# A gated attention and Fourier block: low parts by ScalarE and adding DMAs, M in another place, GpSimd's queue in written order

## The chip, the cores and the metric

The kernel runs on one core of a Trainium2 chip. The core has five engines with queues of their own, each of which works in order: TensorE (PE, matrix products, with its weight loads as PEld), VectorE (DVE), ScalarE (ACT), GpSimd (POOL) and SyncE (SP). SP issues most of the DMAs, GpSimd most of the others. Only semaphores order one engine against another. The metric is the time of one execution on the device in microseconds, as the median of several runs. Lower is better.

## The reference

One input x of 2048 rows and 576 columns feeds two branches, and a gate per row mixes them.

```python
x = A_x
g = _sigmoid((x * gate_w).sum(-1, keepdims=True))
# A: linear attention, 32 heads of 18, phi(t) = where(t > 0, t + 1, exp(t)) + 1e-6
q, k, v = split(x @ wqkv)
kv  = einsum("bhsd,bhse->bhde", phi(k), v);   z = einsum("bhsd->bhd", phi(k))
num = einsum("bhqd,bhde->bhqe", phi(q), kv)
den = einsum("bhqd,bhd->bhq",  phi(q), z)[..., None] + 1e-6
a = (num / den).reshape(B, S, D) @ wo
# B: the real part of a two-dimensional Fourier transform, by matrices
b = dft_seq_re @ (x @ dft_hid_re.T) - dft_seq_im @ (x @ dft_hid_im.T)
return g * a + (1 - g) * b
```

## The kernel before, in words

All products keep float32 accuracy with a matmul type of lower precision. Each operand is split into a high part (ScalarE copies it into that type, `hi_of`, line 179) and a low part (VectorE subtracts the high part from the original, `lo_of`, line 189). A product is then high by high, high by low and low by high. With `lo_later` the subtraction is put on a list, which `tick` empties further on.

The work goes through these stages, with TensorE busy in each:

1. K's features, phi(x Wk), for 16 tiles of 128 rows, with the gate as an extra column (to about 65 us of the span).
2. The product of x transposed with these features, in five chunks of 128 columns of x and four steps each (lines 739 to 772, `step` counts to 19), and kv from it. V itself is never computed.
3. The q stage (lines 1023 to 1029). Row tiles p and p + 8 form a pair. x's quarters are combined with those of Wq so that seven products give four quarters (PRODUCTS, QP). The combinations of x are a pair's *form* (`forms`, seven pieces with high and low part), and the last 64 columns of x a pair's *remainder* (`rests`, in the profile xr). Some forms were made earlier, stored in DRAM (xm) and come back with `load_forms` (xf); those of pairs 6, 0, 7 and 1 are made on the spot from loaded quarters (xb). `Left.make` is that work in five steps: two of additions, the high part, and the low part in two pieces. The pairs come as (6, 2), (3, 4), (0, 5), (7, 1). There are 56 slots, numbered from 0, and each is one product of seven matmuls, the last with the remainder (line 913). Slot 1 is the first of pair 2, slots 24 and 25 the first of pairs 0 and 5, slot 38 the first of pair 7, slot 41 the first of pair 1.
4. In the same stage M is made. M is kv, masked to the heads, times Wo, so that a = (phi(q) / den) M. It is made in five groups of 126 rows (`build_m`, slots 8 to 12, into mf, at the start of the arena), moved by DMA into chunks of 128 rows (`move_m`), and split into high and low part (`split_m`, whose second argument is the part).
5. The M stage: for each of 16 tiles the normalised q features are transposed (line 828), split (qs) and multiplied with M in 28 matmuls. ScalarE scales the result by the gate, and GpSimd stores it (att). The normalising is `normalise`, a generator whose steps (`pz`, the sum per head, the scaling, a copy into `twice`) are called in slots and tiles. In the same tiles the combined weights Wr are loaded and split (`right_raw`, `make_w`) for the next stage.
6. The Fourier branch, real part and then imaginary part: a hidden product (line 1115) and a sequence product (line 1270).

The dictionary `plan` says behind which slot a piece of work is written, and so do the tuples of numbers behind it: for the making of pairs 7, 0 and 1, the normalising steps (None) and M's parts ("m"). ScalarE and VectorE run in written order from line 556 on (`pace`), SP always does, and TensorE does in the q stage and from line 1393 on. Elsewhere a scheduler sets the order at build time, and for GpSimd it does so in the whole kernel before.

All tiles have fixed places in one arena. A write waits until the last readers of whatever lay there are done. Before, M is moved to T_AT + 25856 (`mraw`), where from 28160 on the `sum` tiles of the first quad lie, and its high part goes to T_AT + 14336, where blocks of Wo lay.

Of the kernel before, what the change touches and what calls it, by code (L numbers as in the profile page):

```python
# [8 lines left out]
F = mybir.dt.float32  # L9
# [127 lines left out]
def kernel(  # L137
# [50 lines left out]
    def lo_of(dst, src, hi):  # L188
        nc.vector.tensor_tensor(out=dst, in0=src, in1=hi, op=ALU.subtract)  # L189

# [365 lines left out]
    pace()  # L556
# [154 lines left out]
    def load_forms(p, o, queue=nc.sync):  # L711
        t = forms[p] = at(o, [P, 7, 2, 2 * P], R, "xf")
        for a, b in ((2, 4), (0, 2), (4, 6), (6, 7)):
            queue.dma_start(out=t.bitcast(F)[:, a:b], in_=xforms[p][:, a:b])

    def load_two(*places):
# [89 lines left out]
    def scale(t, d):  # L806
# [3 lines left out]
        o = (SLOT_AT + (14336 if t < 3 else 48256) if t < 4 else T_AT + 36864) + t % 8 * 512  # L810
# [55 lines left out]
    def move_m(g, queue=nc.sync):  # L866

        if not ms:
            ms["raw"] = at(T_AT + 25856, [P, KC, D], F, "mraw")
            ms["rest"] = at(T_AT + 35072, [P, D], F, "mraw")  # L870
        mraw, mrest = ms["raw"], ms["rest"]
# [13 lines left out]

    def split_m(h, part):
        if h == 0 and part == 0:
            ms["hi"] = at(T_AT + 14336, [P, 5, D], R, "mw")
            ms["lo"] = at(T_AT + 25856, [P, KC, D], R, "mw")
        mraw, mrest, mhi, mlo = (ms[k] for k in ("raw", "rest", "hi", "lo"))  # L890
# [91 lines left out]
    def spread():  # L982
        pz_ring.at = [T_AT + 40960 + k * D * 4 for k in range(4)]

    m_parts = [lambda: split_m(0, 0), lambda: split_m(0, 1),
               lambda: split_m(1, 0), lambda: split_m(1, 1)]
# [19 lines left out]
        31: [lambda: load_rest_q(7, T_AT + 80384, nc.gpsimd),  # L1006
             lambda: load_rest_q(1, T_AT + 108928, nc.gpsimd)],
# [15 lines left out]
    with tc.manual_schedule(engines={mybir.EngineType.PE}):  # L1023
        for k, (n, s, q) in enumerate(slots):
# [3 lines left out]
            if k == 51:  # L1028
                nxt = transposed(0)
# [34 lines left out]
    class Hidden:  # L1064
# [12 lines left out]
        def make_w(self, k):  # L1077
# [6 lines left out]
            lo_later(w[:, :, 1], raw, w[:, :, 0])  # L1084
            lo_later(rl[32:64], last[32:64], rl[32:64])
# [239 lines left out]
    for i, t in enumerate(seq):  # L1325
# [12 lines left out]
        if i == 0 or 2 < i < 7:  # L1338
            go(wr_make)
# [3 lines left out]
        for k, j in enumerate((7, 8, 9, 10, 11, 12, 14)):  # L1343
# [149 lines left out]
```

## Time and profile before

| what | value |
|---|---|
| time of the runs, median (lowest to highest) | 731.05 us (730.86 to 732.08) |
| time of the profiled execution | 731.42 us |
| its span, first to last instruction | 729.62 us |
| mean granted clock of TensorE | 0.997 of full speed |
| TensorE busy | 719.6 us, 99% of the span |
| VectorE busy | 597.3 us, 82% |
| ScalarE busy | 329.6 us, 45% |
| GpSimd busy | 56.8 us, 8% |
| moved by DMA | 156.66 MB, on average 215 GB/s |

Times inside the profile count from the start of the span. A row of the timeline has the start, the length, the engine, the line, the operation, what it writes and reads, how many instructions are joined in it, and in brackets how long the engine was idle before it and what ended that.

### The profile page before, as it was taken

Reading aid. Unit: us, or ns where it says so; the run is one execution under the profiler, and the core shown is the slowest. Engines: PE = TensorE matmul, PEld = TensorE weight load, DVE = VectorE, ACT = ScalarE, POOL = GpSimd, SP = SyncE. Lnnn points to the kernel's source line nnn. Section 1 sums busy time; section 2 is a strip of 40 time slices with the busy share of each in tenths; the row PEclk is TensorE's granted clock in tenths of the full one; section 3 lists DMA queues with packets and bytes.
Section 4 is the critical chain, followed back from the end, with each engine's and each line's share of the span. In section 5 each row is a group of like instructions: output and inputs, shape, how many; then the busy total and the mean of one; then the engine's idle time right before and its main releaser. Section 6 shows DMA issues by size and latency. Waiting matters only on the chain.

```text
span 729.6 us, 13716 instructions
## 1 busy us (share of the span) xinstructions
PE 719.6 (99%) x5390; PEld 715.8 (98%) x5390; DVE 597.3 (82%) x996; ACT 329.6 (45%) x506; POOL 56.8 (8%) x101
## 2 busy tenths in 40 slices
PE   9999999998999999999999999999999999999997
PEld 9999999998999999999999999999999999999997
DVE  5799987577999848979999889857888987788884
ACT  6898346575545544443344334323535332232230
POOL 1111221122041100000000000000000000000000
PEclk9999999999999999999999999999999999999999
DMA  7384798984279648454476666889964544544540
GB/s 255 115 279 163 246 302 296 396 276 175 102 260 384 263 147 329 130 161 137 155 247 175 223 240 199 290 308 400 374 198 132 159 140 141 159 150 144 153 152 33
DMA packets 51516, 156.66 MB, mean 215 GB/s; under 512 B 6212, under 2 KB 8676, under 8 KB 50428
## 3 DMA queue, kind: packets, MB, share of 16 engines
q1 hardware_dynamic: 42268, 116.43, 47.3%
q0 software_dynamic: 8896, 38.95, 14.7%
q8 instruction: 43, 0.70, 0.4%
q10 hardware_dynamic: 288, 0.41, 0.2%
q14 instruction: 21, 0.17, 0.1%
HBM read 117.80 MB, written 36.49 MB: 211 GB/s over the span
## 4 chain that ended last, share of the span: by engine, by line
PE 76%; DVE 10%; DMA 9%; issue 2%; ACT 1%; SPq 1%; POOL 1%; DVEq 0%; POOLq 0%; ACTq 0%
PE bank L1270 41%; PE bank L1115 14%; PE bank L209 14%; DMA xr<-xr 2%; DVE c L189 2%; PE bank L913 2%; PE bank L748 2%; PE bank L571 2%; DVE craw L199 1%; DVE fl L189 1%; DMA wraw<-in_wq_rest_dram 1%; DMA craw<-in_xg_dram 1%; DMA xm<-xb 1%; DVE ys L199 1%; PE bank L828 1%
## 5 line engine op out<-in xcount | busy, mean ns | idle before, releaser
L1270 PE MATMUL bank<-fh,c 128*128 128x288 f32 x1792 | 356.1, 295 | 0.4 <-DVE c L189 0.4
L1270 PEld LDWEIGHTS bank<-fh,c 128*128 128x128 f32 x1792 | 286.0, 188 | 1.0 <-DVE c L189 0.9
L1270 PE MATMUL bank<-fl,c 128*128 128x288 f32 x896 | 263.2, 294 | 0.4 <-DVE fl L189 0.4
L179 ACT ACTIVATE c<-craw 128x1792 fp32r<-128x1792 f32 (+1 forms) x84 | 121.6, 1448 | 192.8 <-DVE craw L199 158.4
L1270 PEld LDWEIGHTS bank<-fl,c 128*128 128x128 f32 x896 | 168.7, 188 | 1.1 <-DVE fl L189 0.9
L189 DVE TENSOR_TENSOR c<-craw,c 128x1792 fp32r<-128x1792 f32 (+4 forms) x86 | 141.9, 1653 | 1.7 <-ACT c L179 1.6
L199 DVE TENSOR_TENSOR craw<-craw 128x256 f32<-128x256 f32 (+1 forms) x192 | 98.3, 512 | 24.3 <-DMA craw<-in_ci_dram 13.0
L1115 PE MATMUL bank<-wf,xf 128*128 128x288 f32 x630 | 98.5, 296 | 0.0
L1115 PEld LDWEIGHTS bank<-wf,xf 128*128 128x128 f32 x630 | 90.0, 189 | 0.0
L209 PE MATMUL bank<-mw,qs 128*128 128x288 f32 x448 | 63.5, 298 | 0.8 <-DVE qs L189 0.5
L748 PE MATMUL bank<-pk,c 128*128 128x288 f32 x448 | 62.1, 296 | 0.8 <-ACT c L179 0.4
L748 PEld LDWEIGHTS bank<-pk,c 128*128 128x128 f32 x448 | 60.1, 188 | 1.5 <-DVE c L189 0.8
L209 PEld LDWEIGHTS bank<-mw,qs 128*128 128x128 f32 x448 | 60.0, 188 | 1.4 <-DVE qs L189 0.7
L209 PE MATMUL bank<-wd,xs 128*128 128x288 f32 (+1 forms) x336 | 44.7, 295 | 0.0
L209 PEld LDWEIGHTS bank<-wd,xs 128*128 128x128 f32 x336 | 44.6, 188 | 0.0
L199 DVE TENSOR_TENSOR ys<-bank,ys 128x288 f32<-128x288 f32 x63 | 28.8, 456 | 17.3 <-PE bank L1270 14.3
L189 DVE TENSOR_TENSOR fl<-fl,fh 128x864 fp32r<-128x864 f32 (+1 forms) x32 | 34.6, 1092 | 6.8 <-ACT fh L179 5.2
L179 ACT ACTIVATE fh<-fl 128x864 fp32r<-128x864 f32 (+1 forms) x32 | 29.8, 949 | 16.2 <-DVE fl L199 16.2
L1115 PE MATMUL bank<-wf,xr 96*128 96x288 f32 x112 | 33.3, 298 | 0.0
L199 DVE TENSOR_TENSOR ys<-ys,bank 128x288 f32<-128x288 f32 x47 | 21.1, 450 | 13.5 <-PE bank L1270 12.9
L1292 ACT ACTIVATE ys<-bank 128x288 f32<-128x288 f32 x16 | 6.6, 412 | 53.2 <-PE bank L1270 53.2
L1333 ACT ACTIVATE acc<-bank,gate 128x288 f32<-128x288 f32 x32 | 15.9, 502 | 29.7 <-PE bank L209 29.6
(131 smaller groups left out, 802.1 us busy)
## 6 DMA issues: line engine op xcount, KB each, us to landing
xf<-xm SPq DMA_DIRECT2D x49, 512.0 KB, 9.0
craw<-in_cr_dram SPq DMA_DIRECT2D x32, 512.0 KB, 3.8
craw<-in_ci_dram SPq DMA_DIRECT2D x32, 512.0 KB, 4.2
xr<-xr SPq DMA_DIRECT2D x20, 448.0 KB, 8.2
xm<-xb POOLq DMA_DIRECT2D x8, 1024.0 KB, 5.2
xm<-xb POOLq DMA_DIRECT2D x8, 768.0 KB, 7.1
craw<-in_xg_dram SPq DMA_DIRECT2D x20, 256.0 KB, 5.9
att<-acc POOLq DMA_DIRECT2D x16, 288.0 KB, 3.5
```

Of the source, the lines that this page charges most:

```text
L179: return nc.scalar.activation(dst, src, AF.Copy, bias=bias)
L189: nc.vector.tensor_tensor(out=dst, in0=src, in1=hi, op=ALU.subtract)
L199: nc.vector.tensor_tensor(out=dst, in0=a, in1=b, op=op)
L209: nc.tensor.matmul(ps, a, b, start=(n == 0), stop=(n == len(pairs) - 1))
L571: nc.tensor.matmul(ps[i], x[:, i * P:(i + 1) * P], wkt.row(h, j), start=(c == 0 and n == 0), stop=(c == KC and n == 1))
L748: nc.tensor.matmul(ps[h][:, :HALF], t[:, a, k], pk[s][:, b, half(h)], start=(s == 0 and n == 0), stop=(s == NT - 1 and n == len(passes) - 1))
L828: nc.tensor.transpose(banks[c // KC][:, (c % KC) * P:(c % KC + 1) * P], a, ident)
L913: nc.tensor.matmul(ps, a, b, start=(start and n == 0), stop=(stop and n == len(ops) - 1), skip_group_check=True)
L1115: nc.tensor.matmul(ps, a, b, start=(start and n == 0), stop=(n == len(ops) - 1), skip_group_check=True)
L1270: nc.tensor.matmul(ps[q], c[x][:, l, k], factors[p](y, f), start=(p == 0 and i == 0), stop=(p == NP - 1 and i == 2))
L1292: nc.scalar.activation(c11, ps[1], AF.Copy)
L1333: done.append(nc.scalar.activation(acc[i][:, half(h)], ps[:, :HALF], AF.Copy, scale=gate[:, t:t + 1]))
```

## The change

There are five parts.

- *A new way to a low part.* `lo_by_dma` has ScalarE write the negative of the high part into the place of the low part. A DMA on GpSimd then adds the original to it. `make_w` uses it for the seven weights Wr, at once and no longer by way of the list.
- *M elsewhere.* M is moved straight to where its low part will be, T_AT + 14336, which held blocks of Wo. The high part goes to T_AT + 25856 and is made in two halves of two chunks each, plus the remainder. The negative of each half is written to a place of its own (`minus`), and a DMA adds it to the original, in place. The remainder goes by `lo_by_dma`. The ring of `pz` tiles has two places instead of four once it is spread, and `twice` has another place.
- *GpSimd in written order*, by the argument to the `pace` call of line 556.
- *Loads on other queues.* Remainders 2 and 5 go from SP to GpSimd, remainders 7 and 1 from GpSimd to SP.
- *New slots.* Form 2 is loaded two steps of stage 2 later. The move of M is written behind slot 14 (before 18 and 19), form 5's load behind 15 (before 13), the load for pair 1's form behind 16 (before 19). The making, normalising and splitting steps have new slots, and the first transposition stands behind slot 52 (before 51).

```diff
+    def lo_by_dma(dst, src, hi):
+        nc.scalar.activation(dst, hi, AF.Copy, scale=-1.0)
+        nc.gpsimd.dma_start(out=dst.bitcast(F), in_=src, accum_op=ALU.add)
...
-    pace()
+    pace(mybir.EngineType.Pool)
...
-        14: [lambda: load_forms(2, ACC_AT + 8448, nc.gpsimd), lambda: load_wo(3)],
-        16: [lambda: wo_split[2](lo_later), lambda: load_rest_q(6, SLOT_AT + 40320)],
-        17: [lambda: wo_split[3](lo_later), lambda: load_rest_q(2, SLOT_AT + 43904)],
+        14: [lambda: load_wo(3)],
+        16: [lambda: wo_split[2](lo_later), lambda: load_rest_q(6, SLOT_AT + 40320),
+             lambda: load_rest_q(2, SLOT_AT + 43904, nc.gpsimd),
+             lambda: load_forms(2, ACC_AT + 8448)],
+        17: [lambda: wo_split[3](lo_later)],
...
-        o = (SLOT_AT + (14336 if t < 3 else 48256) if t < 4 else T_AT + 36864) + t % 8 * 512
+        o = (SLOT_AT + (14336 if t < 3 else 48256) if t < 4 else T_AT + 38912) + t % 4 * 512
...
-            ms["raw"] = at(T_AT + 25856, [P, KC, D], F, "mraw")
-            ms["rest"] = at(T_AT + 35072, [P, D], F, "mraw")
+            ms["lo"] = at(T_AT + 14336, [P, KC, D], R, "mw")
+            ms["rest"] = at(T_AT + 23552, [P, D], F, "mraw")
...
+    minus = [at(T_AT + o, [P, 2, D], F, "minus") for o in (45568, 60416)]
...
+            ms["hi"] = at(T_AT + 25856, [P, 5, D], R, "mw")
+        mraw, mrest, mhi = ms["lo"].bitcast(F), ms["rest"], ms["hi"]
+        cs = slice(2 * h, 2 * h + 2)
         if part == 0:
-            hi_of(mhi[:, :KC, half(h)], mraw[:, :, half(h)])
-            hi_of(mhi[:, KC, half(h)], mrest[:, half(h)])
+            hi_of(mhi[:, cs], mraw[:, cs])
+        elif part == 1:
+            nc.scalar.activation(minus[h], mhi[:, cs], AF.Copy, scale=-1.0)
+            nc.gpsimd.dma_start(out=mraw[:, cs], in_=minus[h], accum_op=ALU.add)
         else:
-            lo_of(mlo[:, :, half(h)], mraw[:, :, half(h)], mhi[:, :KC, half(h)])
-            lo_of(mhi[64:, KC, half(h)], mrest[64:, half(h)], mhi[64:, KC, half(h)])
+            hi_of(mhi[:, KC], mrest)
+            lo_by_dma(mhi[64:, KC], mrest[64:], mhi[64:, KC])
...
-        pz_ring.at = [T_AT + 40960 + k * D * 4 for k in range(4)]
-    m_parts = [lambda: split_m(0, 0), lambda: split_m(0, 1),
-               lambda: split_m(1, 0), lambda: split_m(1, 1)]
+        pz_ring.at = [T_AT + 40960 + k * D * 4 for k in range(2)]
+    m_parts = [lambda a=a: split_m(*a) for a in ((0, 0), (1, 0), (0, 1), (1, 1), (0, 2))]
...
-        13: [lambda: load_forms(5, T_AT + 66048, nc.gpsimd)],
-        15: [lambda: load_rest_q(0, SLOT_AT + 40320), lambda: load_rest_q(5, SLOT_AT + 43904)],
-        18: [lambda: move_m(2), lambda: move_m(0, nc.gpsimd), lambda: move_m(3)],
-        19: [lambda: move_m(4), lambda: move_m(1, nc.gpsimd), lambda: begin_left(1, T_AT)],
+        14: [lambda: move_m(2), lambda: move_m(0, nc.gpsimd), lambda: move_m(3), lambda: move_m(4),
+             lambda: move_m(1, nc.gpsimd)],
+        15: [lambda: load_rest_q(0, SLOT_AT + 40320),
+             lambda: load_rest_q(5, SLOT_AT + 43904, nc.gpsimd),
+             lambda: load_forms(5, T_AT + 66048)],
+        16: [lambda: begin_left(1, T_AT)],
...
-        31: [lambda: load_rest_q(7, T_AT + 80384, nc.gpsimd),
-             lambda: load_rest_q(1, T_AT + 108928, nc.gpsimd)],
+        31: [lambda: load_rest_q(7, T_AT + 80384), lambda: load_rest_q(1, T_AT + 108928)],
...
-    for k, what in ((7, (10, 11, 13, 15, 17)), (0, (14, 16, 18, 20, 24)), (1, (33, 34, 35, 36, 38)),
-                    (None, (25, 27, 29, 41, 43, 45, 47, 48, 49, 52)), ("m", (30, 31, 45, 46))):
+    for k, what in ((7, (10, 11, 12, 15, 17)), (0, (13, 15, 17, 19, 23)), (1, (30, 33, 34, 36, 38)),
+                    (None, (18, 20, 25, 35, 41, 43, 47, 48, 48)), ("m", (21, 24, 30, 32, 28))):
...
-            if k == 51:
+            if k == 52:
                 nxt = transposed(0)
...
-            lo_later(w[:, :, 1], raw, w[:, :, 0])
-            lo_later(rl[32:64], last[32:64], rl[32:64])
+            lo_by_dma(w[:, :, 1], raw, w[:, :, 0])
+            lo_by_dma(rl[32:64], last[32:64], rl[32:64])
...
-        for k, j in enumerate((7, 8, 9, 10, 11, 12, 14)):
+        for k, j in enumerate((7, 8, 9, 10, 11, 13, 14)):
```

On GpSimd, from the load of pair 5's form to the stores before the M stage, the rows before are these. xf is form 5, mf is M as it was made, mraw where it is moved, xb_2107 the quarters of pair 1, xr_2251 and xr_2253 remainders 7 and 1, xm the store of a form.

```order
L714 DMA xf_2013<-xm_111 128x1024 x3
L714 DMA xf_2013<-xm_111 128x512
L880 DMA mraw_2081<-mf_1741 112x576
L880 DMA mraw_2081<-mf_1741 14x576
L880 DMA mraw_2081<-mf_1741 2x576
L880 DMA mraw_2081<-mf_1741 112x576
L880 DMA mraw_2081<-mf_1741 12x576
L366 DMA xb_2107<-in_xq_dram 128x2x256 x2
L709 DMA xr_2251<-xr_114 96x896
L395 DMA xm_112<-xb_1260 128x2048
L395 DMA xm_112<-xb_1260 128x1536
L709 DMA xr_2253<-xr_114 128x896
```

Of the changed kernel, at the same place, with xr_2060 as remainder 5, xf_2062 as form 5 and xb_2081 as pair 1's quarters:

```order
L887 DMA mw_2031<-mf_1741 112x576
L887 DMA mw_2031<-mf_1741 12x576
L714 DMA xr_2060<-xr_114 128x896
L719 DMA xf_2062<-xm_111 128x1024 x3
L719 DMA xf_2062<-xm_111 128x512
L371 DMA xb_2081<-in_xq_dram 128x2x256 x2
L400 DMA xm_112<-xb_1260 128x2048
L400 DMA xm_112<-xb_1260 128x1536
L194 DMA mw_2135<-mraw_2032 64x576
L904 DMA mw_2031<-minus_1742 128x1152
L904 DMA mw_2031<-minus_1743 128x1152
```

The move of M went ahead of form 5 and remainder 5, remainders 7 and 1 left the queue, and three adding DMAs came in behind the store of form 6.

On SP, at the move of M, before (xr_2045 and xr_2047 are remainders 0 and 5):

```order
L709 DMA xr_2045<-xr_114 128x896
L709 DMA xr_2047<-xr_114 128x896
L880 DMA mraw_2081<-mf_1741 4x576
L880 DMA mraw_2081<-mf_1741 112x576
L880 DMA mraw_2081<-mf_1741 10x576
L880 DMA mraw_2081<-mf_1741 6x576
L880 DMA mraw_2081<-mf_1741 112x576
L880 DMA mraw_2081<-mf_1741 8x576 x2
L882 DMA mraw_2082<-mf_1741 64x576
L883 DMA mraw_2082<-mf_1741 64x576
```

And in the changed kernel (xr_2058, xr_2259 and xr_2261 are remainders 0, 7 and 1):

```order
L887 DMA mw_2031<-mf_1741 112x576
L887 DMA mw_2031<-mf_1741 8x576 x2
L889 DMA mraw_2032<-mf_1741 64x576
L890 DMA mraw_2032<-mf_1741 64x576
L714 DMA xr_2058<-xr_114 128x896
L714 DMA xr_2259<-xr_114 96x896
L714 DMA xr_2261<-xr_114 128x896
```

Remainder 0 now stands behind the whole move, and remainders 7 and 1 behind that.

On VectorE, before, around the making of pair 1's form (xb_2107 and xb_2108; `acc` are features, `sum` and `pz` as above):

```order
L791 SCALAR_TENSOR_TENSOR pz_2225<-acc_91,zb_984 128x576
L923 SCALAR_TENSOR_TENSOR acc_94<-e_2222,sum_1943 128x288
L923 SCALAR_TENSOR_TENSOR acc_96<-e_2236,sum_1944 128x288
L189 TENSOR_TENSOR mw_2239<-mraw_2081,mw_2238 128x4x288
L189 TENSOR_TENSOR mw_2238<-mraw_2082,mw_2238 64x288
L199 TENSOR_TENSOR xb_2107<-xb_2107 128x256 x4
L199 TENSOR_TENSOR sum_1939<-bank,sum_1939 128x288
L199 TENSOR_TENSOR sum_1940<-bank,sum_1940 128x288
L199 TENSOR_TENSOR sum_1937<-bank,sum_1937 128x288
L189 TENSOR_TENSOR xb_2108<-xb_2107,xb_2108 128x4x256
```

And in the changed kernel (xb_2081 and xb_2082):

```order
L934 SCALAR_TENSOR_TENSOR acc_94<-e_2232,sum_1945 128x288
L204 TENSOR_TENSOR xb_2081<-xb_2081 128x256 x2
L934 SCALAR_TENSOR_TENSOR acc_96<-e_2244,sum_1946 128x288
L204 TENSOR_TENSOR xb_2081<-xb_2081 128x256 x2
L204 TENSOR_TENSOR sum_1941<-bank,sum_1941 128x288
L804 TENSOR_REDUCE den_2105<-pz_2188 128x32
L204 TENSOR_TENSOR sum_1942<-bank,sum_1942 128x288
L204 TENSOR_TENSOR sum_1939<-bank,sum_1939 128x288
L189 TENSOR_TENSOR xb_2082<-xb_2081,xb_2082 128x4x256
```

M's subtractions are gone, and the additions for pair 1's form are split in two pieces, the first of them earlier.

More of the change, by code (lines that the diff above doesn't have):

```diff
@@ L868, in move_m @@
         if not ms:
[L869 to L871 removed]
+            ms["lo"] = at(T_AT + 14336, [P, KC, D], R, "mw")
+            ms["rest"] = at(T_AT + 23552, [P, D], F, "mraw")
+        mraw, mrest = ms["lo"].bitcast(F), ms["rest"]
         row, end = g * GW, g * GW + gsize(g)
@@ L884, in move_m @@
             row += k
+    minus = [at(T_AT + o, [P, 2, D], F, "minus") for o in (45568, 60416)]
     def split_m(h, part):
[L887 to L890, printed above, removed]
+        if not part and not h:
+            ms["hi"] = at(T_AT + 25856, [P, 5, D], R, "mw")
+        mraw, mrest, mhi = ms["lo"].bitcast(F), ms["rest"], ms["hi"]
+        cs = slice(2 * h, 2 * h + 2)
         if part == 0:
-            hi_of(mhi[:, :KC, half(h)], mraw[:, :, half(h)])
-            hi_of(mhi[:, KC, half(h)], mrest[:, half(h)])
-        else:
-            lo_of(mlo[:, :, half(h)], mraw[:, :, half(h)], mhi[:, :KC, half(h)])
-            lo_of(mhi[64:, KC, half(h)], mrest[64:, half(h)], mhi[64:, KC, half(h)])
+            hi_of(mhi[:, cs], mraw[:, cs])
+        elif part == 1:
+            nc.scalar.activation(minus[h], mhi[:, cs], AF.Copy, scale=-1.0)
+            nc.gpsimd.dma_start(out=mraw[:, cs], in_=minus[h], accum_op=ALU.add)
+        else:
+            hi_of(mhi[:, KC], mrest)
+            lo_by_dma(mhi[64:, KC], mrest[64:], mhi[64:, KC])
     def m_row(h, j):
@@ L1337 @@
         tick()
-        if i == 0 or 2 < i < 7:
+        if i in (0, 3, 4, 5, 6):
             go(wr_make)
```

6 lines of the change are left out of this document (3 added, 3 removed).

## The prediction

> **What bounds the kernel now.** I read the page's first part, the waits of TensorE, TensorE's timeline around each wait, and the chain that ended last backwards from there. TensorE is busy nearly throughout, so an edit can gain only what TensorE loses waiting or running slowly.
>
> ```profile
> PE 719.6 (99%) x5390; PEld 715.8 (98%) x5390; DVE 597.3 (82%) x996; ACT 329.6 (45%) x506; POOL 56.8 (8%) x101
> ```
> ```profile
> PE bank L913 <- DVE xb L189: 1.1, 1, 1.1
> PE bank L913 <- DMA xr<-xr: 1.1, 2, 0.8
> PE bank L209 <- DVE qs L189: 0.5, 1, 0.5
> ```
>
> The timeline of TensorE shows what each wait costs: the rows are the start, the length, the work, and in brackets the wait. A slot is seven matmuls.
>
> ```profile
> 132.06 0.96 PE L913 MATMUL bank<-wb,xf 128*128 128x288 f32 x6
> 133.37 0.40 PE L913 MATMUL bank<-wb,xr 96*128 96x288 f32 x1 [0.35 <-DMA xr<-xr]
> 133.60 0.96 PE L913 MATMUL bank<-wb,xb 128*128 128x288 f32 x6
> ...
> 159.27 0.96 PE L913 MATMUL bank<-wb,xb 128*128 128x288 f32 x6
> ...
> 160.21 0.97 PE L913 MATMUL bank<-wb,xf 128*128 128x288 f32 x6
> ...
> 175.18 0.42 PE L913 MATMUL bank<-wb,xb 128*128 128x288 f32 x2
> 176.75 0.82 PE L913 MATMUL bank<-wb,xb 128*128 128x288 f32 x4 [1.15 <-DVE xb L189]
> 178.35 0.40 PE L913 MATMUL bank<-wb,xr 96*128 96x288 f32 x1 [0.79 <-DMA xr<-xr]
> ...
> 182.92 0.96 PE L913 MATMUL bank<-wb,xb 128*128 128x288 f32 x6
> ...
> 194.17 4.15 PE L209 MATMUL bank<-mw,qs 128*128 128x288 f32 x28
> 198.16 0.60 PE L828 MATMUL bank<-ident,acc 128*128 128x128 f32 x4
> ...
> 203.77 0.60 PE L828 MATMUL bank<-ident,acc 128*128 128x128 f32 x4
> ...
> 208.03 0.60 PE L828 MATMUL bank<-ident,acc 128*128 128x128 f32 x4
> ```
> ```profile
> 178.00:180.00 2.00, 1.65 (x9) 1.65 (x10) 2.00 (x5) 1.63 (x5) 0.00 (x0) 0.76 0.00 0
> 180.00:182.00 2.00, 2.00 (x10) 2.00 (x10) 2.00 (x6) 0.94 (x3) 0.00 (x0) 0.50 0.00 0
> ```
>
> An undisturbed slot takes 0.94 us (159.27 to 160.21). There are three losses. Slot 1 took 133.60 - 132.06 = 1.54, so 0.6 was lost on pair 2's remainder. Slots 41 to 44 took 182.92 - 175.18 = 7.74 instead of 3.76, so 4.0 was lost. Only 1.94 of that is idle; the rest is the granted clock, the last but two column of the windows, which falls to 0.76 and then 0.50 after the wait. So a wait near 2 us costs about double. The second M tile took 203.77 - 198.16 = 5.61 where the third took 4.26, so 1.35 was lost. Together that is 5.95 us, the most that this part can give.
>
> Where the large loss comes from is in the chain, the timelines of GpSimd and of the SP queue, and that of VectorE:
>
> ```profile
> 123.15 10.17 DMA xr<-xr
> ...
> 162.19 3.85 DMA mraw<-mf
> ...
> 166.81 0.64 POOL xb L366
> ...
> 170.38 7.93 DMA xr<-xr
> ```
> ```profile
> 121.71 2.16 POOL L714 DMA_DIRECT2D xf<-xm  x4 [16.72 <-DMA wraw<-in_wo_dram]
> ...
> 149.45 2.17 POOL L714 DMA_DIRECT2D xf<-xm  x4 [8.14 <-PE bank L209]
> 156.78 2.65 POOL L880 DMA_DIRECT2D mraw<-mf  x5 [5.16 <-DVE acc L923]
> ```
> ```profile
> 151.02 1.25 SPq L709 DMA_DIRECT2D xr<-xr  x2
> 156.50 5.07 SPq L880 DMA_DIRECT2D mraw<-mf  x7
> ```
> ```profile
> 158.10 1.22 DVE L189 TENSOR_TENSOR xb<-xb,xb 128x1024 fp32r<-128x1024 f32 x1 [0.77 <-ACT xb L179]
> ...
> 167.94 1.85 DVE L189 TENSOR_TENSOR mw<-mraw,mw 128x1152 fp32r<-128x1152 f32 x2 [0.49 <-ACT mw L179]
> 171.91 1.56 DVE L199 TENSOR_TENSOR xb<-xb 128x256 f32<-128x256 f32 x4 [2.12 <-issue]
> ...
> 175.47 1.23 DVE L189 TENSOR_TENSOR xb<-xb,xb 128x1024 fp32r<-128x1024 f32 x1 [0.91 <-ACT xb L179]
> ```
>
> M's move starts at 156.5, because it waits for features (acc L923) whose `sum` tiles lie under mraw. It lands at 166.0, and only then may pair 1's form be loaded over mf (166.8). Its additions begin at 171.9 and its low part ends at 176.7, after slot 41 wants it. Pair 1's remainder stands on GpSimd behind the same load and lands at 178.3.
>
> **The change, part by part.**
>
> *Slots 41 to 44.* M now lands where Wo lay, which needs no `sum` tile. What holds it is slot 12's work on M, which ends at 148.97, slot 13's start:
>
> ```profile
> 148.97 0.95 PE L913 MATMUL bank<-wb,xf 128*128 128x288 f32 x6
> ```
>
> The first of the nine moves on SP needs Wo's second block read, one slot and one block of M earlier (148.97 - 0.94 - 0.8 = 147.2). At 0.72 each (5.07 / 7) the last is issued by 154 and lands near 158 (3.85). Pair 1's form is then loaded at 158 instead of 166.8 and has come by 163 (171.9 - 166.8 = 5.1 later), nine us sooner; its additions (slots 30 and 33), high part (34) and low part (36) follow the slots, so the low part ends near 173, before 175.2. Remainders 7 and 1 go to SP, where they wait only for slots 28 and 29 (159.27 + 5 and + 6 slots of 0.94: 164.0 and 164.9); at the 7.93 of the row they land by 172 and 173, and slots 38 and 41 want them at their last matmul, about 173 and 176. I take the whole loss away: -4.0. The ends are 0 (the form is still late) and -4.0.
>
> *Slot 1.* Remainder 2 went out second on SP and took 10.17. On GpSimd it goes out at the same moment, 122.8, ahead of form 2, whose first piece slips from 121.7 to about 123.4. At 8 us (between 7.93 and 10.17, nearer the first, since it leads its queue) it lands by 131 and form 2 by 131.5, in time for 132.06. -0.6; ends -0.6 and +1.1, the first piece taking 10.17 too. The Trainium skill ("DMA: Bandwidth & Descriptors", section "Issuing engines are not separate DMA queues") says that DMAs of all issuing engines run on the same 16 engines, so that another issuer saves issue time only. By it this term would be nothing and the sum -4.4; the trace cannot decide, since here the load also moves ahead of form 2.
>
> *The first M tiles.* Behind slot 41 VectorE loses M's second subtraction (like the 1.85 of the first), the low part of form 1 (1.23 and a smaller rest of about 0.95), now done before, and two normalising steps, one moved ahead of slot 41 and one behind the second tile: 4.0 and about 1.3. Against that, TensorE arrives 4 us sooner. That leaves about 1 us of air, so I take half of 1.35: -0.7; ends 0 and -1.35.
>
> *Slot 24.* Pair 0's low part ended at 159.3 (158.10 + 1.22) just before the third matmul of the slot from 159.27. Its steps come a slot earlier, but a `pz` step now stands before it on VectorE, and TensorE is 0.6 earlier. I charge +0.3; ends 0 and +1.
>
> *M's low parts.* ScalarE makes M's high part in three copies and the negatives in three, where two pairs stood:
>
> ```profile
> 166.75 1.49 ACT L179 ACTIVATE mw<-mraw 128x1152 fp32r<-128x1152 f32 x2
> ```
>
> By width (1.49 for 1152 and 288 columns) the four wide ones take about 1.1 each and the two narrow ones 0.6, 5.6 us against 3.0, spread over slots 21 to 32 of an engine that is busy 45% of the span. Three adding DMAs go out on GpSimd with slots 28 to 32, about 166 to 170, behind the store of form 6, and the first M tile is due at 194.17 - 5 = 189. No row shows an adding DMA. The nearest are these:
>
> ```profile
> mraw<-mf POOLq DMA_DIRECT2D x2, 252.0 KB, 4.6
> ...
> xf<-xm SPq DMA_DIRECT2D x2, 768.0 KB, 12.3
> ```
>
> The ends are 4.6, and twice 12.3 if reading its target doubles the worst landing. I take about 9, nearer the first, the same kind of copy with twice the bytes; then it is hidden by the 19 us of slots between. If that cover is gone, the delay is paid in full.
>
> *Wr's low parts.*
>
> ```profile
> L189 DVE TENSOR_TENSOR wf<-wraw,wf 128x576 fp32r<-128x576 f32 x7 | 5.3, 752 | 3.4 <-ACT wf L179 3.4
> ```
> ```profile
> 204.00:263.00 59.00, 59.00 (x459) 59.00 (x458) 48.55 (x100) 29.89 (x73) 10.38 (x20) 1.00 0.73 280
> ```
>
> VectorE is freed of these seven and their small ones, and ScalarE gets as many copies; TensorE is busy for all 59 us, so this gains nothing. The last weight is the tight one:
>
> ```profile
> 259.71 1.00 ACT L179 ACTIVATE wf<-wraw 128x576 fp32r<-128x576 f32 x2
> ...
> 268.47 0.96 PE L1115 MATMUL bank<-wf,xb 128*128 128x288 f32 x6
> ```
>
> Copies end at 260.7, negatives about 261.7, and at 4.6 the add lands near 267, before 268.5: 0. At twice that it lands at 271. The swap of `twice` and `pz` places and GpSimd's written order elsewhere move no due work that I can find: 0.
>
> Sum: -4.0 - 0.6 - 0.7 + 0.3 = -5.0 against the profiled run of 731.42 (its span 729.62 and 1.8 around it): 726.4. The median of the runs, 731.05, is 0.4 lower, which I leave as room for small new waits.
>
> **The rivals.**
>
> *Loads late at slots 24 and 25.* Remainder 0 now stands on SP behind nine moves, so it is issued at 154 instead of 151.0, and form 5 behind five moves and remainder 5 on GpSimd, which waits for slot 15: about 152.4 instead of 149.45. With 5 us they make 159.5; with 8 they miss by 2.5, which with the clock costs 4 to 5. Time: 728 to 731. For it speaks the 7.93; against it, that M's bytes have mostly gone by then.
>
> *The adding DMA is slow in the last weight.* At 9.2 (twice 4.6) slot w6 waits 2 us and loses 4: 730.4.
>
> *Slower: M's low parts miss the first M tile.* It decides from a landing about 20 us after issue. At 24.6 from 169 they land at 193.6, 4.6 late, and with the cold clock 7 us are lost: 733.4. For it speaks only that no row prices such a DMA; against it, every copy of this size seen.
>
> *The form is late anyway.* If ScalarE's six copies, in its order ahead of form 1's high part, push that back by over 2 us, the 4.0 stay: 730.4, no change.
>
> **How the numbers follow.** Chances: forecast 0.50 (725 to 728 its own range), late loads 0.20, last weight 0.08, M's low parts 0.12, form late 0.10. Differences under 0.2% (1.5 us) cannot be told from none. Faster, under 729.6: 0.48 of the forecast, 0.15 of the late loads, 0.03 and 0.02 of the weight and the form, 0.68. Slower, over 732.5: the 0.12, and 0.06 for the upper ends of the others. Same: 0.14. The range reaches from all losses gone, 725.1 and a little less, up to 732.5, which leaves out the slower case.
>
> **What would show it.** Right: M's move ends before 159; pair 1's load stands near 158; no TensorE wait at L913 with xb or xr after 170, clock 1.00 throughout 170 to 190; adding DMAs landing within 10 us. Wrong: a wait at the slots after 159, at the first M product, or at the seventh weight near 268; or ScalarE late for `sum` copies.

## The result, and the profile after

The changed kernel takes 735.79 us (median; 734.76 to 736.49), the kernel before 730.95 us. The ratio is 1.0067, with an interval of 1.0049 to 1.0084: slower by 0.67%, where 726.4 was predicted. The profiled execution took 736.08 us, its span 734.4 us. One run of experiment 1, its only profiled one, and one of experiment 9 took 993 and 1168 us at a granted clock of 0.66 and 0.56, and are left out of the ratios below.

The page's first part, of the changed kernel:

```profile
PE 720.6 (98%) x5390; PEld 718.0 (98%) x5390; DVE 586.4 (80%) x978; ACT 340.5 (46%) x522; POOL 74.4 (10%) x118
```

GpSimd is busy for 74.4 us instead of 56.8. TensorE's timeline at the places of the prediction (slot 24; slots 41 and 45; the second and the third M tile; the last M tile):

```profile
159.40 0.96 PE L924 MATMUL bank<-wb,xb 128*128 128x288 f32 x6
163.79 0.47 PE L924 MATMUL bank<-wb,xr 96*128 96x288 f32 x1 [3.43 <-DMA xr<-xr]
164.06 1.64 PE L924 MATMUL bank<-wb,xf 128*128 128x288 f32 x6
...
167.41 0.82 PE L924 MATMUL bank<-wb,xf 128*128 128x288 f32 x5
...
180.50 0.96 PE L924 MATMUL bank<-wb,xb 128*128 128x288 f32 x6
...
184.23 0.97 PE L924 MATMUL bank<-wb,xb 128*128 128x288 f32 x6
...
199.26 0.60 PE L835 MATMUL bank<-ident,acc 128*128 128x128 f32 x4
...
203.51 0.60 PE L835 MATMUL bank<-ident,acc 128*128 128x128 f32 x4
...
255.09 3.95 PE L214 MATMUL bank<-mw,qs 128*128 128x288 f32 x28
262.47 0.93 PE L214 MATMUL bank<-mw,qs 128*128 128x288 f32 x4 [3.43 <-ACT qs L179]
263.20 1.64 PE L1126 MATMUL bank<-wf,xb 128*128 128x288 f32 x6
...
269.67 0.97 PE L1126 MATMUL bank<-wf,xb 128*128 128x288 f32 x6
```

The two waits in brackets, of 3.43 us each, are new and are its largest. The windows of TensorE around them; the last column but two is the granted clock:

```profile
160.00:165.00 5.00, 1.57 (x8) 1.34 (x7) 3.36 (x8) 2.09 (x5) 1.46 (x2) 0.90 0.87 321
165.00:170.00 5.00, 5.00 (x31) 5.00 (x31) 2.10 (x5) 3.77 (x8) 0.16 (x1) 0.76 0.16 55
...
259.00:264.00 5.00, 1.57 (x9) 1.53 (x9) 1.05 (x4) 3.11 (x7) 3.74 (x5) 0.90 0.77 184
264.00:269.00 5.00, 5.00 (x31) 5.00 (x31) 0.00 (x0) 2.54 (x5) 3.48 (x5) 0.76 0.75 181
```

What the prediction promised came. Slots 41 to 44 take 184.23 - 180.50 = 3.73 instead of 7.74, the second M tile 203.51 - 199.26 = 4.25 instead of 5.61, and slot 1's wait is gone. But slots 24 to 26 take 167.41 - 159.40 = 8.01 where three undisturbed slots take 2.81: 5.2 lost, 3.43 of them idle, the rest at a lower clock (six matmuls take 1.64 instead of 0.96). And from the end of the last tile but one, 255.09 + 3.95 = 259.04, to 269.67 there are 10.6 us for one tile and two hidden products, about 5.6 of work: 5.0 lost. Ahead of all that, slot 1 begins at 132.8 instead of 132.06, 0.7 later. So +0.7 - 0.6 + 5.2 - 4.0 - 1.6 + 5.0 = +4.7, and the spans differ by 4.8.

**The first new wait.** The chain that ended last, where it passes slot 24, and the SP queue's timeline at M's move:

```profile
148.37 6.46 DMA mw<-mf
...
154.84 0.02 SPq L714
...
154.89 8.86 DMA xr<-xr
...
163.79 6.32 PE bank L924 x34
```
```profile
147.59 5.49 SPq L887 DMA_DIRECT2D mw<-mf  x7
```

Remainder 0 stands on SP behind the nine moves, the first of which were issued at 147.59. It goes out at 154.89 and takes 8.86; TensorE wants it at 160.4, where the wait in brackets begins. In the kernel before, the remainders 0 and 5 went out from 151.02 on, and the landing that the profile has for them took 8.1.

**The second.** The timelines of GpSimd and of ScalarE before the last M tile, and the DMA issues between 228 and 240 us (count, size of each, time from issue to landing):

```profile
231.76 2.10 POOL L194 DMA_DIRECT2D wf<-wraw  x2 [1.03 <-ACT wf L193]
...
242.21 2.11 POOL L194 DMA_DIRECT2D wf<-wraw  x2 [7.15 <-ACT acc L1344]
243.48 1.43 POOL L1346 DMA_DIRECT2D att<-acc  x1
250.94 2.09 POOL L194 DMA_DIRECT2D wf<-wraw  x2 [6.03 <-ACT acc L1344]
...
255.12 2.07 POOL L194 DMA_DIRECT2D wf<-wraw  x2 [1.51 <-PE bank L214]
256.38 1.41 POOL L1346 DMA_DIRECT2D att<-acc  x1
```
```profile
wf<-wraw POOLq DMA_DIRECT2D x1, 288.0 KB, 10.1
```
```profile
260.31 0.44 ACT L179 ACTIVATE wf<-wraw 96x288 fp32r<-96x288 f32 x1 [3.50 <-DMA att<-acc]
...
261.82 0.77 ACT L179 ACTIVATE qs<-bank 128x512 fp32r<-128x512 f32 x2
```

A pair of additions holds GpSimd for 2.1 us, and the next pair goes out only when the pair before it has landed: 231.8 + 10.1 is 241.9, and the second goes out at 242.21. Its operand was ready at 236.0 (ScalarE's negative); the releaser in brackets, work of ScalarE, is only the last one that the profile shows. Behind the additions stand the stores of att. They fall a tile and more behind, the store at 256.38 lands at 260.3, and only then may ScalarE write the sixth weight over the rows that were stored. Behind that copy in ScalarE's order is the copy of qs that the last M tile waits for.

### The profile page after: what moved, and what is told of

Read it like the earlier page. It is cut to its first block, busy times and chain, and to the rows that moved or that the text cites. A ratio compares the mean times of both kernels' runs of the same rounds, so it can differ in the third digit from the quotient of the medians.

```text
span 734.4 us, 13755 instructions
## 1 busy us (share of the span) xinstructions
PE 720.6 (98%) x5390; PEld 718.0 (98%) x5390; DVE 586.4 (80%) x978; ACT 340.5 (46%) x522; POOL 74.4 (10%) x118
## 4 chain that ended last, share of the span: by engine, by line
PE 82%; DVE 7%; DMA 5%; issue 3%; POOL 1%; ACT 1%; SPq 0%; DVEq 0%; POOLq 0%; ACTq 0%
PE bank L1281 40%; PE bank L1126 14%; PE bank L214 12%; PE bank L924 6%; PE bank L755 6%; DVE c L189 3%; PE bank L576 2%; DVE craw L204 1%; DVE fl L189 1%; DMA xr<-xr 1%; DVE ys L204 1%; DMA craw<-in_cr_dram 1%; PE bank L835 1%; DMA mw<-mf 1%; DMA craw<-in_ci_dram 1%
## 5 line engine op out<-in xcount | busy, mean ns | idle before, releaser
L204 DVE TENSOR_TENSOR fl<-bank,y 128x288 f32<-128x288 f32 x48 | 21.7, 451 | 12.0 <-ACT y L1153 7.4
```

Source lines behind the costliest of these rows:

```text
L204: nc.vector.tensor_tensor(out=dst, in0=a, in1=b, op=op)
```

## The experiments

The theory after the first look: two independent faults, remainder 0's place on SP (5.2 us) and GpSimd standing in Wr's additions (5.0 us). The rivals: DMA engines that are full between 140 and 160 us whatever the order, and, for the second, the low parts themselves, the traffic or the serial nature of an addition. Each experiment edits the changed kernel unless said otherwise; experiments are numbered as their labels are, and there is no number 11. The times of the kernel before beside them were 730.4 to 731.3 us. Intervals are of the ratio to it.

### 1. Remainder 0 in front of the move

```diff
-        14: [lambda: move_m(2), ...
-        15: [lambda: load_rest_q(0, SLOT_AT + 40320), ...
+        14: [lambda: load_rest_q(0, SLOT_AT + 40320), lambda: move_m(2), ...
+        15: [...
```

> The changed kernel, with one load moved: remainder 0 is written in front of M's move on SP (behind slot 14) and not behind it. Theory A (remainder 0 is late because it stands behind the move on SP, and its wait at slot 24 with the cold clock behind it costs 5.2 us): it is issued near 151 as before, lands before 160, slots 24 to 26 take 2.8 us again, and the time is about 735.8 - 5.2 = 730.6. The last M tile still loses its 5. Rival B (the DMA engines are full between 140 and 160, so that any order leaves something late): remainder 0, remainder 5 or form 5 still arrives after slot 24 or 25 wants it, and the time stays within 2 us of 735.8.

Measured: 733.10 us, ratio 1.0037 (1.0021 to 1.0052). That is 2.7 less than the changed kernel and not 5.2, between the two theories. The trace is read in experiment 3, which holds this edit.

### 2. Wr's low parts by VectorE

```diff
-            lo_by_dma(w[:, :, 1], raw, w[:, :, 0])
-            lo_by_dma(rl[32:64], last[32:64], rl[32:64])
+            lo_later(w[:, :, 1], raw, w[:, :, 0])
+            lo_later(rl[32:64], last[32:64], rl[32:64])
```

> The changed kernel, with the low parts of the seven weights Wr subtracted by VectorE again, from the list. Theory A (the adding DMAs hold GpSimd's queue, the stores of att behind them go out late, the seventh weight's place is free late, and ScalarE's copy for the last M tile stands behind that weight's copy): the wait of 3.4 us before the last M tile is gone, GpSimd issues every store of att within 1 us of its tile, the time is about 735.8 - 5.0 = 730.8. Rival B (VectorE is short of time in the M stage, and its subtractions make another wait): a part of the 5 stays, as waits on VectorE's qs or twice, 732 to 735. Rival C (the loads of Wr, not the additions, make the stores late): no change.

Measured: 730.78 us, ratio 0.9993 (0.9981 to 1.0004), 5.0 less, as theory A has it. All stores of att take 0.54 us on GpSimd, one a tile, and no wait is left in the M stage. VectorE had the time.

### 3. Both

> Both edits together: remainder 0 in front of M's move, and Wr's low parts by VectorE. If the two waits are independent and nothing else was lost, the sum of both is taken off: 735.8 - 5.2 - 5.0 = 725.6, which is under the kernel before by 5.3 us. If the two share anything (one DMA backlog, one clock state), less than the sum: 727 to 730.

Measured: 729.02 us, ratio 0.9975 (0.9964 to 0.9987). The two edits do not add up: remainder 0's gives 1.8 here. Slots 24 to 26 take 2.8 us again. ScalarE's timeline, and then TensorE's waits, show what took the gain back:

```profile
162.45 1.17 ACT L179 ACTIVATE mw<-mw 128x1152 fp32r<-128x1152 f32 x1 [1.62 <-DMA mw<-mf]
```
```profile
167.67 1.06 PE L924 MATMUL bank<-wb,xb 128*128 128x288 f32 x6 [0.37 <-ACT sum L965]
...
175.28 1.06 PE L924 MATMUL bank<-wb,xf 128*128 128x288 f32 x6 [0.90 <-ACT sum L967]
```

With the remainder in front of it, the move starts 2.4 us later (149.98 against 147.59). ScalarE then stands 1.62 us before M's second high part, and everything behind it in its order, the `sum` copies among them, is late. Slots 27 to 44 take 20.2 us where the changed kernel takes 16.8. So the early move and the early remainder compete for one place on SP; this part of theory A, that 5.2 was to be had for nothing, falls.

### 4. More descriptor space

```diff
-                   dynamic_dma_scratch_size=1024)
+                   dynamic_dma_scratch_size=1856)
```

> The changed kernel, with all additions kept, and the space for the descriptors of GpSimd's DMAs raised from 1024 to 1856 bytes a partition, the most that the arena leaves. Theory A (GpSimd stands because the descriptors of a pair of additions and of a store fill the space, so that the next addition cannot be issued until the pair before it has landed): the idle times of 7.15 and 6.03 us before the second and the third pair of additions go or fall under 2, the stores of att go out in time, and the last M tile's wait with its cold clock goes: about 730.8. Rival B (an addition cannot be issued before the earlier one has landed, whatever space there is): both idle times stay, 735.8.

Measured: 731.21 us, ratio 1.0009 (0.9996 to 1.0021), 4.6 less, with all additions kept. GpSimd's timeline, and the DMA issues from 229 to 233.9 us:

```profile
232.05 2.10 POOL L194 DMA_DIRECT2D wf<-wraw  x2 [1.14 <-ACT wf L193]
...
236.22 2.08 POOL L194 DMA_DIRECT2D wf<-wraw  x2 [1.01 <-ACT wf L193]
...
242.61 2.06 POOL L194 DMA_DIRECT2D wf<-wraw  x2 [2.96 <-ACT acc L1344]
```
```profile
wf<-wraw POOLq DMA_DIRECT2D x1, 288.0 KB, 10.3
```

The second pair goes out at 236.22, six microseconds before the first has landed (232.05 + 10.3 = 242.4). So an addition need not wait for the one before: rival B falls. The third pair stands, until just that landing. With 1.8 times the space two pairs are under way instead of one, which is what theory A asks for; the descriptors themselves are in no view. The Trainium skill ("DMA: Bandwidth & Descriptors", section "SWDGE vs HWDGE vs iDMA") says that the descriptors of GpSimd's DMAs are written to rings in SBUF. The runs agree in that more such space lets more DMAs be under way; that GpSimd stands for 7.15 and 6.03 us when the space is short is seen in these runs.

### 5. Remainder 0 on GpSimd, Wr by VectorE

```diff
-        15: [lambda: load_rest_q(0, SLOT_AT + 40320),
+        15: [lambda: load_rest_q(0, SLOT_AT + 40320, nc.gpsimd),
              lambda: load_rest_q(5, SLOT_AT + 43904, nc.gpsimd),
```

and the edit of experiment 2.

> Wr's low parts by VectorE, as in the second experiment, M's move where the change put it, and remainder 0 on GpSimd, in front of remainder 5, so that neither the move nor the remainder stands behind the other. Theory A (on SP the two are in each other's way: behind the move the remainder costs 5.2, in front of it it puts M 2.5 us later and ScalarE's copies of M with it): remainder 0 goes out near 150, slots 24 to 26 take 2.8, slots 33 to 45 take 11.2 as in the changed kernel, not 14.6, and the time is 730.8 - 5.5 = 725.3. Rival B (the loads between 145 and 160 share a full set of DMA engines, so that remainder 0, remainder 5 or form 5 is late on any queue): a wait stays at slot 24 or 25, 728 to 731.

Measured: 727.47 us, ratio 0.9956 (0.9940 to 0.9971). Slots 27 to 44 take 16.8 again. GpSimd's timeline and TensorE's wait:

```profile
150.28 0.58 POOL L714 DMA_DIRECT2D xr<-xr  x1 [0.68 <-PE bank L924]
...
151.65 0.53 POOL L719 DMA_DIRECT2D xf<-xm  x1
```
```profile
160.57 1.06 PE L924 MATMUL bank<-wb,xf 128*128 128x288 f32 x6 [1.34 <-DMA xf<-xm]
```

Remainder 0 is in time, but now form 5's first piece, issued at 151.65, is 1.34 late. Each theory has its part: the order on SP was one fault, and with that mended the next load is late, because the DMA engines are full there (a share of 0.99 to 1.03 in each window from 140 to 160).

### 6. The same with additions and more space

Remainder 0 on GpSimd, additions kept, 1856 bytes.

> The changed kernel with all additions kept, remainder 0 on GpSimd in front of remainder 5, and 1856 bytes of descriptor space. Theory A (with space enough the additions cost nothing on the path): the same as with VectorE's subtractions, and about 0.7 less for the wait in the product of stage 2 that went with the larger space: 724.6 to 725.3. Rival B (the additions themselves, at 1.3 us of GpSimd each and their reads, still delay a store or a load): 1 us or more above that.

Measured: 727.29 us, ratio 0.9949 (0.9931 to 0.9966), the same as experiment 5, but 1.8 more than experiment 15, which differs only in VectorE's subtractions; the two intervals overlap a little. The last M tile waits for nothing in this profile, so the large cost of the additions is gone with the space. The two profiled executions do not show it: 726.19 here and 727.02 there, where form 5 is later. Behind slot 44 this one takes 1.6 us more (545.8 us from there to the end, 544.2 in experiment 15), 1.1 of it in short waits of the sequence products, 1.3 against 0.2. Experiment 3, without these additions, has 1.3 of them too, so rival B has its number but is not shown. In any case the additions bring no gain.

### 7. The stores of att by ScalarE

```diff
-        nc.gpsimd.dma_start(out=att[t], in_=acc[i])
+        nc.scalar.dma_start(out=att[t], in_=acc[i])
```

> The changed kernel, with the stores of att issued by ScalarE's queue, directly behind the instruction that makes them, and the additions alone on GpSimd. Theory A (the path is: additions hold GpSimd, stores late, the seventh weight's place free late): the stores go out in time, the wait before the last M tile goes, and the time is 735.8 - 5.0 = 730.8, although GpSimd still stands for some us before the second and third pair. Rival B (the low parts themselves are late, not the stores): the wait stays or moves to the first hidden products, 735.

Measured: 742.78 us, ratio 1.0166 (1.0146 to 1.0185): 7 us worse, which neither theory has. ScalarE's timeline:

```profile
232.31 0.77 ACT L179 ACTIVATE qs<-bank 128x512 fp32r<-128x512 f32 x2 [9.35 <-DMA xf<-xm]
```

ScalarE itself stood 9.35 us there and 6.34 us once more at 240, both ended by the landing of a load of form pieces, which ScalarE's work does not read. What ties its stores to that load the trace does not say. The question stays open here and goes to experiment 14.

### 8. Plain copies in place of the additions

```diff
-            lo_by_dma(w[:, :, 1], raw, w[:, :, 0])
-            lo_by_dma(rl[32:64], last[32:64], rl[32:64])
+            for d, r, x in ((w[:, :, 1], raw, w[:, :, 0]), (rl[32:64], last[32:64], rl[32:64])):
+                nc.scalar.activation(d, x, AF.Copy, scale=-1.0)
+                nc.gpsimd.dma_start(out=d.bitcast(F), in_=r)
```

> The changed kernel, with the additions of Wr's low parts replaced by plain copies of the same size at the same place (the addition is left out, so the products with these low parts are those of other numbers; the amount of work is the same). Theory A (an addition takes about twice the descriptors and twice the issue time of a copy): a copy is issued in about 0.6 us instead of 1.3, GpSimd does not stand before the second and third pair, and the time is 730.8 to 731.5. Rival B (it is the amount that is moved and its number of pieces, added or not): the idle times of 7 and 6 us stay, 735 to 736.

Measured: 730.18 us, ratio 1.0000 (0.9988 to 1.0012), 5.6 less. GpSimd's timeline:

```profile
229.82 1.26 POOL L1098 DMA_DIRECT2D wf<-wraw  x2 [0.98 <-ACT wf L1097]
232.56 0.56 POOL L1348 DMA_DIRECT2D att<-acc  x1 [1.47 <-ACT acc L1346]
234.09 1.25 POOL L1098 DMA_DIRECT2D wf<-wraw  x2 [0.97 <-ACT wf L1097]
```

A pair of copies takes 1.25 us of GpSimd where a pair of additions of the same size takes 2.1 (by the means of the groups one takes 0.63 and 1.29), and the second pair goes out before the first has landed (229.82 + 7.9). So theory A holds: it is the addition, not the amount. That an addition takes more descriptors is inferred from the space; the issue time is measured.

### 9. The kernel before, with more descriptor space

> The kernel before, with only the descriptor space raised to 1856 bytes. Theory A (the space matters only where additions fill it): 730.5, no change within 0.2%. Rival B (the space is a gain by itself, in any kernel of this kind): 726 to 729, and then the gain of the fourth experiment does not speak for the additions.

Measured: 729.06 us, ratio 0.9972 (0.9961 to 0.9983). Rival B: the space alone is worth 2.0 us, without any addition. GpSimd's timeline in stage 2, of the kernel before and then of this one:

```profile
72.95 2.18 POOL L372 DMA_DIRECT2D xb<-in_xq_dram  x3 [5.54 <-DVE zacc L199]
76.80 0.72 POOL L372 DMA_DIRECT2D xb<-in_xq_dram  x1 [1.67 <-issue]
```
```profile
72.97 2.88 POOL L372 DMA_DIRECT2D xb<-in_xq_dram  x4 [5.29 <-DVE zacc L199]
```

Four loads in a row did not fit, and the fourth stood 1.67 us (4.12 in the changed kernel, whose written order has a store ahead of them). With the larger space it goes out at once, the waits of stage 2 go, and slot 1 no longer waits for remainder 2, although that is issued by SP as before. Of the gain of experiment 4 the part in the M stage is still the additions': from the end of slot 44 to the end of the span experiment 4 takes 545.4 us, the changed kernel 550.0.

### 10. M's low parts by VectorE as well

Experiment 5, with `lo_of` in place in the slots of the additions.

> The fifth experiment's kernel with M's low parts subtracted in place by VectorE, at the same slots, and not added by DMA. Theory A (taking M's subtractions off VectorE is what removed the loss of the first M tiles, and M's new place alone removed that of slots 41 to 45): the second M tile loses 1 to 1.6 us again, 728.5 to 729.1; slots 41 to 45 stay at 3.7. Rival B (M's early move alone did both): 727.5, no loss at the first M tiles.

Measured: 728.95 us, ratio 0.9963 (0.9948 to 0.9977). The second and the third M tile in TensorE's timeline:

```profile
196.59 0.60 PE L835 MATMUL bank<-ident,acc 128*128 128x128 f32 x4
...
200.97 0.60 PE L835 MATMUL bank<-ident,acc 128*128 128x128 f32 x4
```

The tile takes 4.38, so at most 0.1 is lost there: rival B by the trace, though the time is theory A's. What is over experiment 5 lies elsewhere, for the most part in slots 24 to 32, where form 5 is 2.2 late in this profile and 1.3 in that. The intervals of the two experiments overlap for the most part, so that their difference is not clear.

### 12 and 13. Remainder 0 in the middle of the move, form 5 first

```diff
-        14: [lambda: move_m(2), lambda: move_m(0, nc.gpsimd), lambda: move_m(3), ...
+        14: [lambda: move_m(2), lambda: move_m(0, nc.gpsimd),
+             lambda: load_rest_q(0, SLOT_AT + 40320), lambda: move_m(3), ...
-        15: [..., lambda: load_rest_q(5, SLOT_AT + 43904, nc.gpsimd), lambda: load_forms(5, T_AT + 66048)],
+        15: [lambda: load_forms(5, T_AT + 66048), lambda: load_rest_q(5, SLOT_AT + 43904, nc.gpsimd)],
```

and the edit of experiment 2; 13 has the larger space besides.

> Wr's low parts by VectorE; remainder 0 on SP in the middle of M's move, behind its fifth DMA; and on GpSimd form 5 in front of remainder 5. Theory A (what is left of the fifth experiment's loss is form 5's first piece, which was issued at 151.65 behind two remainders and landed 1.34 us late): form 5 goes out near 149.3, slots 24 to 26 take 2.8, M's move ends only half a us later, and the time is 727.5 - 1.6 = 725.9. Rival B (M's end is as tight as the third experiment showed, or remainder 0 is late again): one of the two waits is back, 727 to 729.

> The same with 1856 bytes of descriptor space. Theory A (the space also takes away the wait of 0.7 to 0.9 us in stage 2, where GpSimd's fourth quarter load stood 4 us): about 0.7 to 1 less than the twelfth kernel, 725.1. Rival B (that wait has slack behind it): the same as the twelfth.

Measured: 732.24 us, ratio 1.0018 (1.0007 to 1.0029), and 731.77 us, 1.0009 (0.9996 to 1.0022). GpSimd's timeline of 12, and TensorE's wait:

```profile
153.55 0.54 POOL L714 DMA_DIRECT2D xr<-xr  x1 [0.66 <-DMA mw<-mf]
```
```profile
165.35 0.61 PE L924 MATMUL bank<-wb,xr 96*128 96x288 f32 x1 [5.33 <-DMA xr<-xr]
```

Remainder 0 and form 5 are in time, and remainder 5, now last, goes out at 153.55, takes 11.8 us and is 5.3 late. Rival B, at a higher price than given. In 13 the space brings no more than 0.5, within the intervals: its rival B. With M's move where the change puts it, whichever of the three loads (the two remainders and form 5) went out last missed its slot in every order tried. In experiment 3, where the move starts 2.4 later, all three are in time and M is late.

### 14. The late stores of att by SP

```diff
-        nc.gpsimd.dma_start(out=att[t], in_=acc[i])
+        (nc.sync if i > 8 else nc.gpsimd).dma_start(out=att[t], in_=acc[i])
```

> The changed kernel, with the stores of att from tile 9 on issued by SP, in its written order, and not by GpSimd; all additions and the descriptor space of 1024 bytes stay. Theory A (what the last M tile waits for is the late stores, over whose rows ScalarE's copy for the sixth weight must wait): ScalarE no longer waits for att, the wait of 3.4 us goes, the time is 735.8 - 5.0 = 730.8, whether or not GpSimd still stands before an addition. Rival B (the late low parts, or the additions' own traffic, hold the last tile): the wait stays, or comes at the hidden products, 734 to 736.

Measured: 740.87 us, ratio 1.0127 (1.0102 to 1.0152). The wait of the last M tile is gone, so the stores were what it waited for. But GpSimd still stands before additions, and now TensorE waits for the low parts themselves. GpSimd's timeline, then TensorE's:

```profile
263.00 2.08 POOL L194 DMA_DIRECT2D wf<-wraw  x2 [6.85 <-issue]
271.62 2.11 POOL L194 DMA_DIRECT2D wf<-wraw  x2 [6.54 <-issue]
```
```profile
271.33 1.57 PE L1126 MATMUL bank<-wf,xb 128*128 128x288 f32 x5 [5.62 <-DMA wf<-wraw]
...
275.59 1.57 PE L1126 MATMUL bank<-wf,xb 128*128 128x288 f32 x5 [2.21 <-DMA wf<-wraw]
```

So theory A is right on the wait and wrong on the price, and rival B has the second half: the additions are late enough to miss the hidden products too. How much of that is due to SP's loads, which now come later behind the stores and run beside the last additions, was not tried apart.

### 15. The best of these

Experiment 5 with 1856 bytes.

> The fifth experiment's kernel (Wr's low parts by VectorE, remainder 0 on GpSimd in front of remainder 5) with 1856 bytes of descriptor space. Theory A (the space takes about 1.4 to 2 us off any kernel with these loads, as it did to the kernel before, in stage 2 for the most part): 725.5 to 726.2. Rival B (what the space gave the kernel before was slot 1 and stage 2, which the change already has in part): 726.5 to 727.5, no more than the sixth experiment.

Measured: 725.48 us, ratio 0.9926 (0.9910 to 0.9942), faster than both kernels. Theory A by its time, 2.0 less than experiment 5 (from 12 to 13 it was 0.5). Form 5 is still late in the profile, so more is left; the wait in TensorE's timeline:

```profile
160.53 1.81 PE L924 MATMUL bank<-wb,xf 128*128 128x288 f32 x6 [2.31 <-DMA xf<-xm]
```

## Why the prediction was wrong, point by point

- *Slots 41 to 44, -4.0.* Right in size, and the trace fits the cause: M's early move frees the place of pair 1's form. But that form is loaded at 162.48 and not near 158; the one landing of M's remainder that the profile has took 6.8 us, where the sum had 3.85. The air that was left covered it, also in experiment 5, where the load stands at 162.07 and slot 41 begins only 0.5 later than before (175.63). The early move, the new slots and the other queue of remainders 7 and 1 were not undone one by one. Experiment 3 shows how tight it is, with 3.4 lost behind a move that starts 2.4 later.
- *Slot 1, -0.6.* Right in size. The cause was not tested apart by another queue alone. Experiment 9 reaches the same with remainder 2 on SP, with the remainder issued 1.8 us earlier and slot 1 begun 1.4 earlier, so the wait can go without another issuer. By the rule of the Trainium skill that is cited there ("DMA: Bandwidth & Descriptors", section "Issuing engines are not separate DMA queues") the term would be nothing. Whether the issuer or the place ahead of form 2 took the wait away here stays open.
- *The first M tiles, -0.7.* Right in sign, at half the size (-1.35 on the second tile). Experiment 10 shows that the adding DMAs are not needed for it: VectorE may keep M's subtractions where they are now written, ahead of slot 41. That fits the reason given, less work for VectorE behind slot 41, but nothing tests it apart.
- *Slot 24, +0.3.* Failed. It charged VectorE only and took no term for remainder 0, which I left to a rival with a chance of 0.20. It cost 5.2; the rival had 4 to 5. The row of 7.93 us for such a load stood in the prediction; I set the 5 us of other loads beside it and took that, although the trace before has 8.1 for a remainder on SP at this very place (8.86 came). The argument against the rival, that M's bytes have mostly gone by then, failed too: in the windows from 145 to 160 the DMA share was 0.61, 0.81 and 0.96 before and is 1.01, 0.99 and 1.01 after, because the change brings M's move there.
- *M's low parts, 0.* Right. The additions land in 9.0 to 10.5 us, as I estimated, and TensorE does not wait. The slower case of the prediction rested on these, so the kernel is slower for another reason than the one it gave.
- *Wr's low parts, 0.* Failed, and this turned the sign: 5.0 us. The term priced the addition as something that lands (4.6 to 9.2 us), and looked only for the weight that lands last. What GpSimd has to do to issue it, how many can be under way, and what stands behind it in its queue, the stores of att, were not in the sum. The rival on the last weight looked at the right additions and the wrong wait.
- *GpSimd's written order elsewhere, 0.* Not shown to be wrong. Slot 1 begins 0.7 later than in the kernel before, and in stage 2 the order puts a store ahead of four loads, the fourth of which stands 4.1. But eight other profiles with the same code up to there and the same 1024 bytes (experiments 2, 3, 5, 7, 8, 10, 12 and 14) begin slot 1 at 130.5 to 131.9, all of them earlier than the 132.06 before, so that the 0.7 is within the spread of executions.

With what this pair of profiles shows, the sum is -4.0 - 0.6 - 1.6 + 5.2 + 5.0 + 0.7 = +4.7 on 731.42, which is the 736.1 of the profiled execution; the last term is the late start of slot 1.

## What to carry to other kernels

Price a DMA on three counts: the issuing engine's time, what it leaves of that queue's descriptor space while it is under way, and the landing; then look at what stands behind it in the queue and whose place that frees. Where the change itself fills the DMA engines, a load that is moved behind others should be priced at the longest landing of such a load in the trace, and another one becomes the late one when it is moved back. Before a kernel is rearranged around a queue that stands, try more space for the descriptors: here one number was worth 2 us in the kernel before, with nothing else touched.

## What the runs showed of the hardware that was not expected

- *An adding DMA and descriptor space.* With 1024 bytes one pair of additions (288 KB and 36 KB) is under way at a time (the second goes out at 242.21, when the first has landed), with 1856 two (236.22 and 232.05). Plain copies of the same shape overlap already with 1024 (234.09 and 229.82). A pair of additions takes 2.1 us of GpSimd's time against 1.25.
- *Short waits and the clock.* Over slots 24 to 32, which take 8.4 us undisturbed, a wait of 1.34 us cost 1.6 (experiment 5), one of 1.46 cost 1.7 (6), of 2.23 cost 4.0 (10), of 2.31 cost 3.9 (15), of 3.43 cost 5.2 (the changed kernel) and of 5.33 cost 8.3 (12). So in these profiles, one for each wait, a single wait begins somewhere between 1.5 and 2.2 us to cost 1.6 us and more on top of itself. That is the clock: from 160 to 165 us the granted clock was 1.00 in experiments 5 and 6, 0.78 in 10 and 0.66 in 15. Shorter waits close together do it as well: in the kernel before, 1.15 and 0.79 in slots 41 to 44 cost 4.0. The Trainium skill ("TensorE: Matmul & The Clock Gate", section "What's actually happening") puts the fall of the clock behind an idle window of about 3.4 us; here waits of 2.2 us already bring it.
- *Stores on ScalarE's queue* made ScalarE stand 9.35 and 6.34 us for loads of another queue (experiment 7). The cause stays open.
